# Merging two store transfers into one, a sixth load buffer, and a new fixed order of every engine, in a fused retention and gated feed-forward kernel

## The chip, the cores and the metric

The kernel runs on one core of a Trainium2 chip. The metric is device time in microseconds (us), the median of several executions. The profile is one execution taken by the hardware profiler; its span is about 1 to 2 us shorter than the time of the same run.

Engines are called PE (TensorE matmul), PEld (its weight loads), DVE (VectorE), ACT (ScalarE), POOL (GpSimd) and SP (the queue that issues transfers). An "h_ps" group is the first feed-forward matmul of one tile of 128 tokens, an "o_ps" group the second; there are 36 tiles. An eviction copies a matmul's result into a buffer (o_sb is that of the output). A store or load lands when its completion is reported. The chain is the work that ended last, followed back step by step to what released it. The granted clock is the share of its full clock that PE was allowed.

## The reference

```python
# retention: B=8, H=8, S=576, D=64
scores = (1/8) * q @ k^T
ret    = scores * Dmat           # causal, gamma_h ** (i - j)
x      = (ret @ v), heads side by side        # 4608 tokens x 512
# feed-forward
h    = x @ w_in                                # 512 -> 1024
solu = h * softmax(h)
ln   = (solu - mean) / sqrt(var + 1e-6) * g_ln
out  = ln @ w_out                              # 1024 -> 512, fp32
```

Inputs and the output are fp32: 32.7 MB are read and 9.4 MB written.

## The kernel before

Every instruction is an "op" with an engine, a duration, its dependencies and the buffers that it takes. For each engine a list (`FIRST`) fixes the order of the first 80 to 130 ops; the rest follow a periodic key. A small list scheduler turns this into one program order. So each engine works through a fixed order, and an engine that stands at one op stands with all that follow.

A load takes two neighbouring rows into one partition, so a tile's 128 tokens come out with the parity `j` slow and the pair index `q` fast: row `64*j + q` of the output tile belongs at row `2*q + j` in memory. The store undoes that, by two transfers per full tile, one for each parity:

```python
CAP = dict(raw=5, ..., xT=5, h=1, e=2, oc=2, solu=3, ..., o=1, osb=3)   # buffers
...
def x_ev(i):                                   # xT: the transposed tokens that h_ps reads
    nc.scalar.copy(out=d["xT"].rearrange("p c h q -> p c (h q)"), in_=d["av"][:, :, 0:256])

def o_ev(t):                                   # evicts o_ps into osb, the buffer of the store
    nc.scalar.activation(out=d["osb"], in_=..., func=ACT.Copy, scale=...)

def store(t):
    for j in range(2):
        q_dma = nc.scalar if t == NT - 1 and j else nc.sync
        if wi < 2:                             # a full tile: 32 of the 36
            r0 = b * S + 256 * wi + P * c
            q_dma.dma_start(
                out=out[r0 : r0 + P, :].rearrange("(q j) m -> j q m", j=2)[j],
                in_=tk[t]["osb"][64 * j : 64 * j + 64],
            )
        else: ...                              # cut: the 4 tail tiles, four pieces each
```

The softmax here doesn't subtract the row's maximum and nothing guards it: scores larger than these inputs give would overflow.

## Time and profile before

| | before |
|---|---|
| time, median | 225.9 us |
| span of the profile | 224.9 us |
| PE busy, share of the span | 207.0 us, 92% |
| a half-tile store, issue to landing | 2.4 us |
| ACT waiting with an o_sb eviction for a store | not among its waits |

Page of the kernel before: span and busy times, the rows of 40 slices for PE, the granted clock and DMA, the packet counts, the main DMA queue, the chain, and the stores' line of the DMA issues (KB each, us to landing).

```profile
span 224.9 us, 7378 instructions
PE 207.0 (92%) x2985; PEld 121.8 (54%) x2985; DVE 181.5 (81%) x320; ACT 163.2 (73%) x238; POOL 151.8 (67%) x231
...
PE   7776989899699999699999999999999999999991
...
PEclk9999999999999999999999999999999999999998
DMA  6999999995576610799988776777763552222324
...
DMA packets 65635, 42.64 MB, mean 190 GB/s; under 512 B 4024, under 2 KB 59456, under 8 KB 65600
...
q1 hardware_dynamic: 65200, 41.96, 66.9%
...
PE 63%; DVE 17%; DMA 9%; POOL 4%; issue 2%; SPq 2%; ACT 1%; DVEq 0%; POOLq 0%; ACTq 0%
...
out_dram<-o_sb SPq DMA_DIRECT2D x64, 128.0 KB, 2.4
```

PE is busy for 90% or more of each of the last 28 slices but two: the second half is at PE's limit. The chain that ended last is mostly PE's. Gaps are in the first half. The table of windows says so with numbers; the columns are the stretch, its length, busy time (instructions) of each engine, granted clock, DMA share and GB/s:

```profile
43.90:111.40 67.50, 63.32 (x973) 38.41 (x971) 63.96 (x104) 52.74 (x77) 57.16 (x81) 1.00 0.68 187
111.40:201.00 89.60, 89.60 (x1379) 55.12 (x1377) 75.67 (x136) 69.64 (x102) 64.55 (x103) 1.00 0.62 168
```

### The profile page before, as it was taken

What the parts mean: (1) busy time and instruction counts of PE and PEld (TensorE: products, weight loads), DVE (VectorE), ACT (ScalarE), POOL (GpSimd) and SP (SyncE); (2) the same over time, 40 slices, a digit from 0 to 9 for tenths busy, and PEclk for the clock granted to TensorE, in tenths of its full rate; (3) what the DMA queues carried; (4) which work ended last, traced back from release to release, by engine and by line L of the source; (5) the groups of instructions that cost most, each with busy time, mean ns of one, the idle gap of its engine ahead of it and who ended that gap; (6) DMA issues with size and microseconds to landing.
All of it is one profiled execution on the core that took longest, in us unless ns stands there. A gap on an engine that the chain in (4) does not pass through costs nothing.

```text
span 224.9 us, 7378 instructions
## 1 busy us (share of the span) xinstructions
PE 207.0 (92%) x2985; PEld 121.8 (54%) x2985; DVE 181.5 (81%) x320; ACT 163.2 (73%) x238; POOL 151.8 (67%) x231
## 2 busy tenths in 40 slices
PE   7776989899699999699999999999999999999991
PEld 2433445556455556465666666665666666555440
DVE  6654788999999998999999888888887888876540
ACT  3555889776869988578787777777777777776751
POOL 3429599899989989829578869695968677311010
PEclk9999999999999999999999999999999999999998
DMA  6999999995576610799988776777763552222324
GB/s 176 360 344 348 320 262 287 286 279 157 128 224 173 195 24 13 188 305 293 267 235 247 215 195 192 214 191 191 218 184 109 153 131 52 50 47 60 84 69 119
DMA packets 65635, 42.64 MB, mean 190 GB/s; under 512 B 4024, under 2 KB 59456, under 8 KB 65600
## 3 DMA queue, kind: packets, MB, share of 16 engines
q1 hardware_dynamic: 65200, 41.96, 66.9%
q8 instruction: 23, 0.38, 0.8%
q10 hardware_dynamic: 400, 0.21, 0.5%
q14 instruction: 12, 0.10, 0.2%
HBM read 32.71 MB, written 9.44 MB: 187 GB/s over the span
## 4 chain that ended last, share of the span: by engine, by line
PE 63%; DVE 17%; DMA 9%; POOL 4%; issue 2%; SPq 2%; ACT 1%; DVEq 0%; POOLq 0%; ACTq 0%
PE h_ps L431 21%; PE o_ps L501 21%; PE xy L311 6%; PE tln L480 5%; PE tqk L291 4%; DMA qr<-in_q_dram 4%; DVE solu L451 4%; PE s_ps L346 4%; DVE bs L457 3%; DVE ret L379 3%; DMA vr<-in_v_dram 3%; DMA kr<-in_k_dram 2%; DVE oc L509 2%; SPq L259 2%; DVE w L465 1%
## 5 line engine op out<-in xcount | busy, mean ns | idle before, releaser
L431 PE MATMUL h_ps<-w_in_122,xT 128*128 128x512 f16 x288 | 68.0, 379 | 2.0 <-DVE solu L451 1.9
L451 DVE TENSOR_TENSOR solu<-h_ps,e_sb 128x1024 f16<-128x1024 f32 x36 | 43.9, 1219 | 13.4 <-ACT e_sb L444 13.2
L444 ACT ACTIVATE e_sb<-h_ps 128x1024 f32<-128x1024 f32 x36 | 36.8, 1022 | 18.2 <-PE h_ps L431 17.9
L457 DVE BATCH_NORM_STATS2 bs<-solu 128x6 f32<-128x512 f16 x72 | 46.0, 680 | 0.1
L379 DVE TENSOR_TENSOR ret<-s_ps,masks 128x1024 f16<-128x1024 f32 x36 | 43.7, 1215 | 0.6 <-PE s_ps L346 0.4
L299 ACT COPY qkT<-tqk 128x1024 f16<-128x1024 f16 x36 | 36.3, 1008 | 9.3 <-PE tqk L291 9.1
L431 PEld LDWEIGHTS <-xT 128*128 128x128 f16 x288 | 27.0, 98 | 29.1 <-issue 2.8
L501 PEld LDWEIGHTS <-lnT 128*128 128x128 f16 x288 | 25.9, 98 | 27.2
L488 ACT COPY lnT<-tln 128x1024 f16<-128x1024 f16 x36 | 36.2, 1005 | 3.5 <-PE tln L480 3.5
L501 PE MATMUL o_ps<-w2c_124,lnT 128*128 128x512 f16 x160 | 38.0, 380 | 0.0
L501 PE MATMUL o_ps<-w2g_123,lnT 128*128 128x512 f16 x112 | 26.5, 380 | 0.0
L419 ACT CAST xT<-xy 128x512 f16<-128x512 f32 x36 | 21.4, 594 | 6.6 <-PE xy L311 6.2
L404 POOL TENSOR_TENSOR g<-tt,small 128x128 f32<-128x128 f32 x32 | 13.4, 418 | 15.3 <-DVE tt L400 15.3
L480 PEld LDWEIGHTS <-solu 128*128 128x128 f16 x288 | 18.5, 98 | 8.7 <-DVE solu L451 1.7
L517 ACT ACTIVATE o_sb<-o_ps,rs 128x512 f32<-128x512 f32 x20 | 13.7, 687 | 12.7 <-PE o_ps L501 6.9
L480 PE MATMUL tln<-ident,solu 128*128 128x128 f16 x288 | 22.0, 219 | 0.9 <-DVE solu L451 0.9
L346 PE MATMUL s_ps<-qkT 64*64 64x128 f16 x576 | 14.9, 220 | 0.8 <-ACT qkT L299 0.7
L346 PEld LDWEIGHTS <-qkT 64*64 64x64 f16 x576 | 9.5, 107 | 4.6 <-ACT qkT L299 1.8
L395 DVE TENSOR_TENSOR g<-xy,g 128x128 f32<-128x128 f32 x16 | 4.6, 289 | 8.7 <-PE xy L311 5.2
L400 DVE TENSOR_TENSOR tt<-xy,g 128x128 f32<-128x128 f32 x32 | 9.3, 292 | 2.7 <-ACT xT L419 0.7
L509 DVE SCALAR_TENSOR_TENSOR oc<-nws,mv,o_ps 128x512 f32<-128x512 f32 x14 | 10.3, 738 | 0.2 <-PE o_ps L501 0.2
L517 ACT ACTIVATE o_sb<-oc,rs 128x512 f32<-128x512 f32 x14 | 10.2, 728 | 0.3 <-DMA qr<-in_q_dram 0.3
(507 smaller groups left out, 336.9 us busy)
## 6 DMA issues: line engine op xcount, KB each, us to landing
kr<-in_k_dram SPq DMA_DIRECT2D x32, 256.0 KB, 4.6
vr<-in_v_dram SPq DMA_DIRECT2D x32, 256.0 KB, 4.8
qr<-in_q_dram SPq DMA_DIRECT2D x32, 256.0 KB, 4.8
out_dram<-o_sb SPq DMA_DIRECT2D x64, 128.0 KB, 2.4
w_in_f<-in_moe_w_in_dram SPq DMA_DIRECT2D x4, 512.0 KB, 5.9
w_f<-in_moe_w_out_dram SPq DMA_DIRECT2D x4, 512.0 KB, 8.0
qr<-in_q_dram SPq DMA_DIRECT2D x16, 64.0 KB, 2.3
kr<-in_k_dram SPq DMA_DIRECT2D x16, 64.0 KB, 2.0
```

Of the source, the lines that this page charges most:

```text
L299: nc.scalar.copy(out=d["qkT"], in_=d["tp"])
L346: nc.tensor.matmul(out=sv[ee[c], e, hp, j], lhsT=qkT[ee[e], 1, hp, j, ee[c]], rhs=qkT[ee[e], 0, hp, :, ee[c]], start=True, stop=True,)
L379: nc.vector.tensor_tensor(out=d["ret"].rearrange("p e h j q -> p (e h) (j q)"), in0=d["s"].rearrange("p e h j q -> p (e h) (j q)"), in1=ma ...
L419: nc.scalar.copy(out=d["xT"].rearrange("p c h q -> p c (h q)"), in_=d["av"][:, :, 0:256])
L431: nc.tensor.matmul(out=h_ps[:, hh], lhsT=st[2 * w + dc // 2]["xT"][:, c, dc % 2], rhs=w_in16[:, dc, hh], start=(dc == 0), stop=(dc == 3),)
L444: nc.scalar.activation(out=d["e"], in_=d["h"], func=ACT.Exp, accum_out=ws[w]["se"][:, c : c + 1])
L451: nc.vector.tensor_tensor(out=d["solu"], in0=d["h"], in1=d["e"], op=ALU.mult)
L457: nc.vector.bn_stats(out=bs[:, half], in_=tk[t]["solu"][:, half * 512 : half * 512 + 512])
L480: nc.tensor.transpose(out=tp[:, c], in_=d["solu"][:, c * P : (c + 1) * P], identity=ident)
L488: nc.scalar.copy(out=d["lnT"], in_=d["tp"])
L501: nc.tensor.matmul(out=d["o"], lhsT=d["lnT"][:, c], rhs=(w2g16 if t < NE else w2c16)[:, c], start=(c == 0), stop=(c == 7))
L517: nc.scalar.activation(out=d["osb"], in_=d["oc"] if t < NE else d["o"], func=ACT.Copy, scale=ws[t // 2]["rs"][:, t % 2 : t % 2 + 1],)
```

## The change

Its intent: save the second issue of each full tile's store; let loads run further ahead (`raw` from 5 to 6); and replace the order by a new one, listed over the whole run instead of about the first half of each engine's ops. A transposing load of k is also in the code, but its threshold (`ND = 99`) leaves it unused.

```diff
-    CAP = dict(raw=5, qk16=3, v16=4, tp=1, qkT=3, s=1, ...
+    CAP = dict(raw=6, qk16=3, v16=4, tp=1, qkT=3, kT=3, s=1, ...
 FIRST = dict(
     PE=(
-        "G K0 T0 S0 T1 I0 V0 K1 S1 I1 V1 M1_0 T2 K2 S2 L0 I2 V2 K3 T3 M1_1 S3 WM ..."
+        "G T0 K0 S0 T1 I0 V0 K1 S1 I1 V1 M1_0 T2 K2 S2 T3 M1_1 I2 V2 K3 S3 L0 ..."
         ... (cut: all five engines, to the last op of the run)
     def store(t):
-        for j in range(2):
-            q_dma = nc.scalar if t == NT - 1 and j else nc.sync
-            if wi < 2:
-                r0 = b * S + 256 * wi + P * c
-                q_dma.dma_start(
-                    out=out[r0 : r0 + P, :].rearrange("(q j) m -> j q m", j=2)[j],
-                    in_=tk[t]["osb"][64 * j : 64 * j + 64],
-                )
+        if wi < 2:
+            r0 = b * S + 256 * wi + P * c
+            nc.sync.dma_start(
+                out=out[r0 : r0 + P, :].rearrange("(q j) m -> j q m", j=2), in_=tk[t]["osb"]
+            )
         ... (cut: the 4 tail tiles, four pieces each as before)
```

## The prediction

> **What bounds the kernel now.** TensorE. The page gives PE 207.0 of 224.9 us (92%) at full granted clock. In the table of windows PE is busy 89.6 of 89.6 us between 111.4 and 201 us; successive h_ps groups (one per 128-token tile, 36 in all) start 5.26 to 5.37 us apart there. No order of the same instructions shortens that stretch. PE idle, plus warm-up matmuls of zeros counted as busy:
>
> - 15.6 to 24.2 us (first to second h_ps): 2.5 + 1.2
> - 24.2 to 31.1: 1.0 + 0.6
> - 31.1 to 43.9: 0.9
> - 43.9 to 111.4: 4.2
> - 201 to the end: 5.4, of which 4.6 is the last eviction and store.
>
> About 11 us could go at best, none of it in the second half.
>
> **Why those gaps exist.** From 44 to 111 us VectorE is busy 64.0 of 67.5 us: it is the limit there, because the first 14 tiles need an extra pass (oc, 0.74 us). Part of that is blocking: the 2-column adds of line 468 take 0.16 us in the second half but 0.97 to 1.20 us at 47, 58, 92 and 104 us, when GpSimd is mostly busy. The Trainium skill (SBUF — State Buffer, "Who interferes with whom") says a VectorE instruction with two SBUF inputs contends with a GpSimd one reading SBUF; these durations agree. The largest PE wait (1.7 us at 92 us) follows such a pair (0.82 + 1.19 us), placed ahead of the mask that PE needed.
> Before 44 us loading sets the pace: DMA share is about 1.0, and GpSimd waits 2.6 us (at 14 to 17) and 1.5 us (at 26 to 28) for data.
>
> **What the change does.** Transfers: a full tile's two stores (1.11 us of issue together) become one. SP matters only where its in-order queue stands at stores: from 74 to 91 us it issues eight stores while DMA falls to 0.03 share; GpSimd later waits 4.0 us for a q load. The new order spreads stores among loads; the sixth buffer lets loads run further ahead. Neither is worth more than about 0.5 us directly. The DMA transpose code is dead (its threshold is 99). No work is removed, apart from about three warm-up matmuls.
>
> Order: the second h_ps now comes before the attention of tiles 2 and 3, so it should start near 22 us instead of 24.2, the third near 28 to 29 instead of 31.2. But one q load goes ahead of k4's, one more w_out transfer ahead of v3's, and between 31 and 44 us GpSimd has 11.7 of 12.8 us of work and ScalarE 10.9, so most of the lead is paid back: about 1 us (0 to 2.5) remains at the fifth h_ps. From 44 to 111 us better interleaving can win at most VectorE's idle and blocking: I take 2.3 us (0.5 to 3.5). Steady part: 0 to -0.3. End: within 0.5. Sum: about 3.7 us.
>
> **Predicted:** 222.3 us, 219.3 to 225.0 eight times in ten. Faster by over 2% (under 221.5): 0.37; within 2%: 0.61; slower: 0.02.
>
> **What would show it.** Second h_ps at 21.5 to 23 us; fifth within 41.5 to 44; fifth to seventeenth h_ps 64 to 66 us (67.45 now); the remaining nineteen intervals unchanged at 98.7 us ±0.7; no long SP stand at stores between 70 and 95 us.
>
> **What would make it wrong.** Faster: the early lead is kept because loads arrive sooner than GpSimd needs them, or VectorE's blocking vanishes. Slower: the order does not know the blocking by GpSimd or DMA queueing, and one engine standing at a late operand stops the others; or stalls appear in the now-fixed second half.

## The result, and the profile after

The changed kernel takes 282.8 us (median of 4 runs, 282.4 to 283.4) against 225.9 us. The ratio is 1.252, with a 95% interval of 1.248 to 1.256. Ratios here are the mean time of one kernel's runs over that of the other's of the same rounds, so not quite the ratio of the medians quoted.

Page of the changed kernel, the same lines as above:

```profile
span 281.6 us, 7301 instructions
PE 220.5 (78%) x2982; PEld 126.2 (45%) x2982; DVE 178.2 (63%) x320; ACT 163.5 (58%) x238; POOL 151.7 (54%) x231
...
PE   8588999929999665994269879899496899999600
...
PEclk9999999977999997999859997999779999999985
DMA  8999996585443453648424345664331111111122
...
DMA packets 64674, 42.63 MB, mean 151 GB/s; under 512 B 3064, under 2 KB 58496, under 8 KB 64640
...
q1 hardware_dynamic: 64240, 41.95, 49.2%
...
DMA 50%; PE 21%; SPq 10%; ACT 10%; issue 3%; POOL 2%; DVE 0%; ACTq 0%; POOLq 0%
DMA out_dram<-o_sb 38%; SPq L293 7%; PE o_ps L545 7%; PE h_ps L475 6%; DMA kr<-in_k_dram 5%; DMA w_f<-in_moe_w_out_dram 3%; DMA qr<-in_q_dram 3%; PE tqk L333 3%; ACT e_sb L488 2%; ACT lnT L532 2%; ACT qkT L342 2%; PE tln L524 2%; PE xy L354 2%; ACT o_sb L561 2%; DMA masks<-masks 2%
...
out_dram<-o_sb SPq DMA_DIRECT2D x32, 256.0 KB
```

The compute work is the same (ACT 163.5 us against 163.2; PE is busy for 13.5 us more, at a mean granted clock of 0.93), but half of the chain is now DMA, and stores are 38% of the chain. PE has holes until about the 225th us and at the end, and its granted clock dips around many of them. Yet the DMA row is emptier than before. The stores' line gives no time to landing here; landings below are those of the chain. The waits of ACT name the place (us in total, times, longest):

```profile
ACT o_sb L561 <- DMA out_dram<-o_sb: 55.1, 17, 8.6
```

One such hole, in the chain in order of time (start, length):

```profile
78.75 7.86 DMA qr<-in_q_dram
...
86.70 7.86 DMA out_dram<-o_sb
...
94.66 0.04 ACT o_sb L561
...
95.29 1.10 ACT e_sb L488 x2
96.39 0.41 ACT lnT L532
96.80 8.68 DMA out_dram<-o_sb
```

A store is issued at 86.70 us and lands at 94.56. Only then does ACT get an `osb` buffer (there are three), evict o_sb, and go on in its fixed order to the exponential and to lnT, for which PE waits. In this view the store takes 7.9 us, three times as long as each half before, for twice the bytes. The q load ahead of it in the chain takes 7.86 us too, against a median of 4.8 us before.

The chain does not say why it is slow. The packet line does. "Under 512 B" counts, beside small data, the 4-byte packets that report a transfer's completion. They fall by 4024 - 3064 = 960. With 16 of them for each of the 64 half stores of before and 2 for each of the 32 single stores of now, the fall is 64 × 16 - 32 × 2 = 960. So each single store ran on 2 DMA engines. The Trainium skill (DMA: Bandwidth & Descriptors, "Why a DMA increments its semaphore by 16 and not by 1") states the rule: such a transfer uses the largest number of engines, at most 16, that divides the slowest dimension of size above 1 on both sides, and each engine used posts one completion. The new store's output pattern is `j q m`, with j = 2 outermost. The old halves had q = 64 there.

The packet records say it a second way. I took every 2 KB packet from the first store's to the last one's (the w_out loads, whose packets have that size too, are over by then) and counted how many are in flight at once, as shares of that time:

```
in flight               0      1      2      3     4 to 13   14 to 17
before                65.3%   4.0%   1.5%   1.1%    14%        14%
changed kernel        23.0%   5.9%  62.3%   6.3%    1.7%       0.7%
```

The 2.4% with four or more come almost wholly from the tail tiles, whose pieces are cut as before. In the last stretch of the changed kernel, where nothing but stores flows, two or three are in flight nearly without a break. With packets of every kind counted (over 100 bytes, from the 30th us to the end), fewer than two are in flight for 1.3% of the time in the changed kernel and for 23.9% before: as it should be if two engines hardly ever rest. The records do not name the engine, so this is not a count per engine. It also fits the length of the run. The main queue takes 49.2% of 16 × 281.6 us, so 2217 engine-us. The full tiles' stores are 32 × 128 packets of 84 ns median, 344 engine-us, half on each of the two engines: 172 us. The rest, spread over 16, is about 117 us for each engine. An estimate from these: 172 + 117 = 289 us of work for each of those two engines, in a span of 281.6 us (a little too much; three store packets at once on two engines mean that the records of neighbouring packets overlap). By this estimate they are full, while the other 14 are busy for 117 us. It takes the loads to fill them: from 225 to 257 us, with the loads over, PE is busy 31.8 of 32 us in the changed kernel, so in that stretch stores alone on two engines keep up with PE.

### The profile page after: what moved, and what is told of

The parts are those of the page before. It is cut to its first block, busy times and chain, and to the rows that moved or that the text cites. A ratio compares the mean times of both kernels' runs of the same rounds, so it can differ in the third digit from the quotient of the medians.

```text
span 281.6 us, 7301 instructions
## 1 busy us (share of the span) xinstructions
PE 220.5 (78%) x2982; PEld 126.2 (45%) x2982; DVE 178.2 (63%) x320; ACT 163.5 (58%) x238; POOL 151.7 (54%) x231
## 2 busy tenths in 40 slices
DMA packets 64674, 42.63 MB, mean 151 GB/s; under 512 B 3064, under 2 KB 58496, under 8 KB 64640
## 3 DMA queue, kind: packets, MB, share of 16 engines
q1 hardware_dynamic: 64240, 41.95, 49.2%
## 4 chain that ended last, share of the span: by engine, by line
DMA 50%; PE 21%; SPq 10%; ACT 10%; issue 3%; POOL 2%; DVE 0%; ACTq 0%; POOLq 0%
DMA out_dram<-o_sb 38%; SPq L293 7%; PE o_ps L545 7%; PE h_ps L475 6%; DMA kr<-in_k_dram 5%; DMA w_f<-in_moe_w_out_dram 3%; DMA qr<-in_q_dram 3%; PE tqk L333 3%; ACT e_sb L488 2%; ACT lnT L532 2%; ACT qkT L342 2%; PE tln L524 2%; PE xy L354 2%; ACT o_sb L561 2%; DMA masks<-masks 2%
## 5 line engine op out<-in xcount | busy, mean ns | idle before, releaser
L475 PE MATMUL h_ps<-w_in_125,xT 128*128 128x512 f16 x288 | 70.7, 390 | 0.4 <-DVE solu L495 0.3
L545 PE MATMUL o_ps<-w2c_127,lnT 128*128 128x512 f16 x160 | 40.8, 401 | 1.7 <-ACT o_sb L561 0.9
L545 PEld LDWEIGHTS <-lnT 128*128 128x128 f16 x288 | 27.5, 102 | 30.9 <-issue 5.4
L475 PEld LDWEIGHTS <-xT 128*128 128x128 f16 x288 | 27.8, 100 | 29.3 <-issue 3.7
L545 PE MATMUL o_ps<-w2g_126,lnT 128*128 128x512 f16 x112 | 28.1, 397 | 0.0
L463 ACT CAST xT<-xy 128x512 f16<-128x512 f32 x36 | 21.2, 588 | 11.4 <-DVE tt L444 6.4
L524 PE MATMUL tln<-ident,solu 128*128 128x128 f16 x288 | 23.5, 227 | 4.7 <-ACT lnT L532 4.1
L437 DVE COPY g<-xy 128x128 f32<-128x128 f32 x16 | 4.6, 290 | 13.5 <-PE xy L354 13.3
```

The source lines that it names most:

```text
L475: nc.tensor.matmul(out=h_ps[:, hh], lhsT=st[2 * w + dc // 2]["xT"][:, c, dc % 2], rhs=w_in16[:, dc, hh], start=(dc == 0), stop=(dc == 3),)
L524: nc.tensor.transpose(out=tp[:, c], in_=d["solu"][:, c * P : (c + 1) * P], identity=ident)
L545: nc.tensor.matmul(out=d["o"], lhsT=d["lnT"][:, c], rhs=(w2g16 if t < NE else w2c16)[:, c], start=(c == 0), stop=(c == 7))
```

## The experiments

Theory T1: the single store runs on 2 engines because of its outermost size, and these two cannot carry the stores and their share of the loads. Rivals: T2, the new order itself makes engines stand; T3, one transfer per tile is slow because it is one (a larger piece that frees its buffer later). All runs of one batch share a chip. The kernel before took a median of 226.1 us beside the first four, 225.8 us beside the others.

### 1. Only the stores undone (a_two_stores)

```diff
 # changed kernel, store(): the two half-tile transfers of the kernel before
# (cut: the tail tiles' four pieces go back to their old order too)
-        nc.sync.dma_start(out=... "(q j) m -> j q m" ..., in_=tk[t]["osb"])
+        for j in range(2):
+            q_dma.dma_start(out=... "(q j) m -> j q m" ...[j], in_=tk[t]["osb"][64*j : 64*j+64])
```

> The changed kernel with only the stores put back to two transfers per full tile (one for even, one for odd output rows). Theory T1 (the single store names the row parity, of size 2, as its slowest dimension and so runs on 2 of the 16 DMA engines): 219 to 225 us, o_sb no longer waits for store DMA (55 us in the changed kernel, under 3 us here), TensorE clock back above 0.98. T2 (the new order itself makes engines stand): 270 us or more. T3 (one transfer per tile is slow because it is one, whatever its shape): 219 to 225 us.

Measured: 226.1 us, ratio to before 0.999 (0.995 to 1.003). The small packets are those of the kernel before again, 4024, and the o_sb wait for stores falls from 55.1 to 0.8 us (second line):

```profile
DMA packets 65634, 42.63 MB, mean 190 GB/s; under 512 B 4024, under 2 KB 59456, under 8 KB 65600
...
  DMA out_dram<-o_sb: 0.8, 2
```

So all of the 56.7 us between 282.8 and 226.1 us come from the store. T2 falls. My own number for the new order (219 to 225 us) fails too; section 6 takes that up.

### 2. Only the single store, on the kernel before (b_one_store)

```diff
 # kernel before, store(): the single transfer of the changed kernel
-        for j in range(2): ... two half-tile transfers
+        nc.sync.dma_start(out=... "(q j) m -> j q m" ..., in_=tk[t]["osb"])
```

> The kernel before with only the single store per full tile. T1 and T3: 260 us or more, with o_sb waiting for store DMA some 40 us or more and only about 0.13 DMA share while nothing but stores flows. T2: 225 to 227 us.

Measured: 290.6 us, ratio 1.284 (1.278 to 1.290); o_sb waits 55.2 us for stores. The small packets are as few as in the changed kernel, 3064:

```profile
DMA packets 64674, 42.63 MB, mean 148 GB/s; under 512 B 3064, under 2 KB 58496, under 8 KB 64640
```

The single store alone makes the loss, in either order. The DMA share that I named as a sign was a bad one. While only stores flow it is 0.14 on two engines (changed kernel, first line) and 0.14 on 16 (the changed kernel with a_natural's stores of section 3, second line):

```profile
225.00:257.00 32.00, 31.77 (x390) 17.99 (x387) 24.73 (x42) 23.99 (x35) 8.91 (x17) 1.00 0.14 54
...
190.00:210.00 20.00, 20.00 (x266) 11.59 (x265) 15.11 (x28) 14.85 (x21) 2.56 (x5) 1.00 0.14 50
```

The packets in flight are the sign.

### 3. One store per tile on 16 engines (a_natural, b_natural, a_outer16)

If tokens are put into natural order earlier, when xT is written, the output tile is one contiguous block and its single store has 128 rows outermost. The result is correct.

```diff
 def x_ev(i):
     nc.scalar.copy(
-        out=d["xT"].rearrange("p c h q -> p c (h q)"), in_=d["av"][:, :, 0:256]
+        out=d["xT"].rearrange("p c h (q j) -> p c h j q", j=2),
+        in_=d["av"][:, :, 0:256].rearrange("p c (h j q) -> p c h j q", h=2, j=2),
 def store(t):       # full tiles (cut: the tail tiles, two pieces each in place of four)
+        nc.sync.dma_start(out=out[r0 : r0 + P, :], in_=tk[t]["osb"])
```

> The changed kernel with the tokens put into natural order when xT is evicted (a permuted write on ScalarE), so that the output tile is one contiguous block and its single store has 128 rows as its slowest dimension. Same result. T1: 218 to 225 us, each store landing in 2 to 4 us, xT copy not over 0.65 us. T3: 265 us or more. T2: 270 us or more.

> The kernel before with natural token order (permuted xT copy) and so one 16-engine store per full tile. The issue of stores is not on the chain: 225.5 to 227.5 us; the xT copy at 0.74 us instead of 0.59 us, as in the same edit of the changed kernel. A gain of 1% or more would show that store issue mattered in the kernel before.

Measured: 227.7 us on the changed kernel (ratio 1.004, 0.999 to 1.009) and 227.4 us on the kernel before (1.004, 0.998 to 1.010). Stores of 256 KB land in 2.2 us. T3 falls: one transfer per tile is as good as two when it has 16 engines. It is not better. The chain of the kernel before has no store's issue in it; the dearer copy below could hide a small gain, but a_outer16 (section 5), which has one store per tile without that copy, takes 226.5 us and is no faster either. The permuted copy takes 0.74 us instead of 0.59, which I had expected to be free in the first of the two runs and had not priced.

The DMA issues' line for stores in the changed kernel with natural order:

```profile
out_dram<-o_sb SPq DMA_DIRECT2D x32, 256.0 KB, 2.2
```

### 4. Two transfers, cut the other way (a_col_halves)

```diff
 # changed kernel, full tiles: two transfers of 256 columns, each still "j q m"
+        for m in (slice(0, 256), slice(256, 512)):
+            nc.sync.dma_start(out=out[r0 : r0 + P, m].rearrange("(q j) m -> j q m", j=2),
+                              in_=tk[t]["osb"][:, m])
```

> The changed kernel with two transfers per full tile, cut by columns (256 each), each still naming the row parity first. T1: as slow as the changed kernel or slower, 278 us or more (same two engines, pieces of 1 KB instead of 2 KB). T3: 219 to 230 us, as with the two transfers of before. T2: about 282 us.

Measured: 292.1 us, ratio 1.290. Two transfers again, with the size 2 outermost, and as slow. What the two halves of before had was not their number but their outermost dimension.

### 5. The number of engines as a dose (a_outer4, a_outer8, a_outer16) and the number of buffers (a_osb12, a_outer4_osb12)

The row order is made wrong, so these three give a wrong result; the bytes, the 2 KB pieces and all else are those of the changed kernel. Only the outermost size differs.

```diff
-    out=out[r0 : r0 + P, :].rearrange("(q j) m -> j q m", j=2), in_=tk[t]["osb"]
+    out=out[r0 : r0 + P, :].rearrange("(q a) m -> a q m", a=4), in_=tk[t]["osb"]   # or 8, 16
```

> The changed kernel, still one 256 KB store per full tile and the same 2 KB pieces, but with 4 as the slowest dimension of its output pattern (output row 4q+a instead of 2q+j: the rows of a tile land in the wrong order on purpose, so the result is wrong). T1 as a matter of engine count: per engine about 117 us of other traffic plus half of the 2-engine store time of about 170 us, together near 203 us, under the span that TensorE needs: 226 to 234 us, hardly any o_sb wait for store DMA. If only 16 engines will do, or if the slowness is that of a single strided store: 265 us or more.

> One store per full tile with 8 as the slowest dimension (row order wrong on purpose). T1 by engine count: per engine about 117 us of other traffic plus 43 us of stores; between the 16-way form (226.5 us) and the 4-way form (242.4 us): 226 to 231 us.

> The same with 16 as the slowest dimension (row order wrong on purpose). T1: 225 to 227.5 us, like the changed kernel with two stores; store landing 2 to 3 us. If scattered rows in one transfer were the fault: 265 us or more.

| outermost size | time, us | ratio to before | packets under 512 B |
|---|---|---|---|
| 2 (the changed kernel) | 282.8 | 1.252 | 3064 |
| 4 | 242.4 | 1.069 | 3128 |
| 8 | 227.0 | 1.004 | 3256 |
| 16 | 226.5 | 1.000 | 3512 |

The small packets follow 3000 + 32 × size exactly, so the number of engines used is the outermost size, as the skill's page has it. Time falls with it. (One of the four runs with size 4 counts as slow; the fast ones take 241.2 to 242.9 us.) The scatter of the rows is not what costs: the median 2 KB packet of a store takes 84 ns with each of the four sizes. Eight are enough here; four are not, against my estimate of 226 to 234 us. The packet lines of the changed kernel with size 4 and with size 16:

```profile
DMA packets 64738, 42.63 MB, mean 177 GB/s; under 512 B 3128, under 2 KB 58560, under 8 KB 64704
```

```profile
DMA packets 65122, 42.63 MB, mean 189 GB/s; under 512 B 3512, under 2 KB 58944, under 8 KB 65088
```

More buffers tell lack of throughput from a wait that buffering could hide:

```diff
-               xT=5, h=1, e=2, oc=2, solu=3, sml=8, lnT=4, o=1, osb=3)
+               xT=5, h=1, e=2, oc=2, solu=3, sml=8, lnT=4, o=1, osb=12)
```

> The changed kernel with 12 instead of 3 buffers of o_sb. If two DMA engines lack throughput for stores plus their share of loads (about 117 + 172 us of work in a 282 us run): still 272 to 285 us, the waits moving from o_sb to load data and to the end. If it is only the latency of one store against three buffers: under 240 us.

> The 4-way store (242.4 us, above what I had expected) with 12 o_sb buffers. If four engines have throughput enough (about 203 us of work) and the loss was stores queued behind bursts of loads against three buffers: 225 to 231 us, no o_sb wait for store DMA. If four engines still lack throughput, in the loading half at least: 238 us or more, with waits for load data in place of the o_sb waits.

Measured with size 2: 282.9 us, as with three buffers. The waits of POOL for loads in that run (with three buffers they sum to 9.4 us for v, 7.3 for k and 8.4 for q):

```profile
POOL v L316 <- DMA vr<-in_v_dram: 31.2, 5, 15.2
...
POOL k L308 <- DMA kr<-in_k_dram: 16.9, 7, 4.9
POOL q L308 <- DMA qr<-in_q_dram: 9.4, 5, 5.4
```

ACT no longer waits for stores, and loads come late instead. By the rule cited above each load of 128 rows also has a sixteenth on each of the two full engines, and it has landed only when these have delivered; the records do not show this engine by engine. So the limit is the throughput of two engines, not the wait for a buffer.

Measured with size 4 and twelve buffers: 238.1 us against 242.4. So the buffers gave back 4 of the 16 us above the 16-engine form. The rest is again late loads (POOL waits 12.5 us for v). My estimate for four engines, 203 us of work in the run, is a mean over the run; that stretches of heavy loading exceed it fits the waits but was not measured per engine.

### 6. The new order and the sixth buffer (hyb_two, a_two_raw5)

With two stores the new order takes 226.1 us, no faster than before; I had predicted 222.3. Starts of the h_ps groups in the profiles divide the runs (us):

| | first h_ps | 1st to 5th | 5th to 17th | 17th to 36th | 36th to end | span |
|---|---|---|---|---|---|---|
| before | 15.63 | 28.30 | 67.45 | 98.67 | 14.85 | 224.9 |
| new order, two stores | 16.87 | 26.48 | 68.81 | 99.58 | 12.86 | 224.6 |
| new order in about its first half only | 15.85 | 27.64 | 67.65 | 98.67 | 14.89 | 224.7 |
| new order, two stores, five load buffers | 16.24 | 27.17 | 75.58 | 106.87 | 12.84 | 238.7 |

The last row's profile is of a slow run (240.7 us), and no profile of a fast one is kept.

In the new order PE has done one more o_ps group by the 17th h_ps (14 against 13), and so has one fewer to do after the 36th; a group is 1.73 us. Taking that out, the middle stretch gains 67.45 - (68.81 - 1.73) = 0.37 us and the end 14.85 - 12.86 - 1.73 = 0.26 us. The steady stretch loses 0.91 us. (The first h_ps is late in the second row because PE's clock was granted at half speed from 11 to 17 us in that execution; other runs of this order begin at 15.5 to 16.2 us.)

```diff
 # hyb_two: changed kernel with two stores; FIRST cut to the ops that the kernel before
 # also listed (94 of ACT's, 100 of DVE's, 129 of PE's, 102 of POOL's, 85 of SP's), in the new order
```

> The changed kernel with two stores per full tile and its new order kept only for those instructions whose order the kernel before fixed too; the rest by the periodic rule of before. If fixing the whole run costs what the profile shows (0.9 us more between the 17th and the 36th h_ps than before): that stretch back to 98.4 to 99.0 us and 225.0 to 225.9 us in all. If the two runs merely scatter: 99.3 to 99.9 us there and 226.0 to 226.4 us in all.

Measured: 226.6 us, ratio 1.002 (0.997 to 1.006). The steady stretch is back to 98.67 us, so its 0.9 us did belong to the new late order; but the end takes 14.89 us, and the total is the same. The expected 225.0 to 225.9 us fails, because I had not counted that the extra o_ps group goes back to the end.

Why the middle gave so little: the same stretch, 5th to 17th h_ps, in the kernel before, with the new order, and with the new order in about the first half only.

```profile
43.93:111.38 67.45, 63.27 (x971) 38.36 (x969) 63.91 (x104) 52.71 (x77) 57.12 (x81) 1.00 0.68 187
```

```profile
43.35:112.16 68.81, 65.73 (x981) 39.50 (x979) 62.35 (x106) 53.15 (x78) 61.83 (x89) 1.00 0.83 238
```

```profile
43.49:111.14 67.65, 63.62 (x971) 38.55 (x969) 60.62 (x105) 52.42 (x77) 57.48 (x83) 1.00 0.65 181
```

In the last of them DVE (third busy column) has 3.3 us less to do than before, since fewer of its small adds were blocked by POOL (3.7 us of blocking against 6.7 us, summed over the durations of the two small operations above their usual 0.11 and 0.16 us). The stretch is no shorter. So DVE's work is not shown to bound it, and this run speaks against it. PE leaves the least room: it is busy 63.3 of 67.45 us, so 4.2 us at best could go (that PE is the limit there was not tested by itself). Of these the new order removed 1.1 us of idle time, while its busy time, the extra group taken out, rose by 0.7 us.

The sixth buffer:

```diff
-    CAP = dict(raw=6, ...      # changed kernel with two stores
+    CAP = dict(raw=5, ...
```

> The changed kernel with two stores per full tile and five load buffers as before. If the sixth buffer contributes nothing: 226.0 to 226.8 us, as with six. If the new order leans on it: 228 us or more, with GpSimd waiting for loads.

Measured: 239.3 us (median of 4; two of these runs count as slow, being over 1.5% above the fastest; the fast ones are 236.1 and 238.9, ratio 1.049). So the new order leans on the sixth buffer. The waits of SP's queue, in the profile of a slow run, suggest the way it happens:

```profile
SPq L293 <- POOL k L308: 20.8, 9, 10.2
SPq L293 <- POOL q L308: 12.6, 7, 3.8
```

A load stands at the head of the in-order queue until POOL frees a buffer, and the stores behind it stand too; ACT then waits 11.4 us for stores. No profile of a fast run of this form is kept, so the way is not shown for those.

No version beat the kernel before: 226.1 us (new order, six buffers, two stores) is the nearest, and is the same within the interval.

## Why the prediction was wrong

- **The step that failed** is "Neither is worth more than about 0.5 us directly", said of the merged store and the sixth buffer. I costed the store by its issue time on SP (1.11 us for two) and did not ask whether its landing would change. The runs show 56.7 us for the store alone on the new order (282.8 to 226.1 us) and 64.5 us on the old one (226.1 to 290.6). The output pattern's outermost size went from 64 to 2, and with it the engines from 16 to 2. The diff shows this: the `[j]` behind the rearranged pattern is gone, so j has become a dimension, and the outermost one. The skill's page states the rule; I did not look it up because I read the edit as a saving of issue time.
- The list of what would make the prediction wrong named DMA queueing only for the order. It did not ask which resource the store runs on.
- The sixth buffer: also mis-sized. The new order without it takes 239.3 us against 226.1 us with it. What it is worth in the old order was not run.
- **The middle stretch**, "I take 2.3 us (0.5 to 3.5)", was worth 0.37 us at equal PE work. The step behind it, "it is the limit there", said of VectorE, failed: in hyb_two three microseconds less of its work shortened nothing. A share of 95% busy did not show it to be the limit. The skill's rule on blocking (SBUF — State Buffer, "Who interferes with whom") does fit the 0.16 and 0.97 to 1.20 us of the same add; but in hyb_two 3.0 us less of such blocking did not shorten the stretch.
- The early part held: second h_ps predicted at 21.5 to 23 us, measured 21.74; third at 28 to 29, measured 28.27; fifth within 41.5 to 44, measured 43.41 (in the changed kernel, before its first stores pile up). The last range is a weak test: the kernel before, with 43.93, lies in it too. The total of 222.3 us would have failed without the slow stores as well (226.1 us).
- "The remaining nineteen intervals unchanged at 98.7 us ±0.7" failed: 126.1 us in the changed kernel, 99.6 us with two stores.
- The dips of the granted clock (mean 0.928) come with the holes in PE's work and go with them (0.98 or more in a_two_stores). How much of the 56.7 us they add was not separated; PE's busy time rose by 13.5 us.

## What to carry to other kernels

When transfers are merged or a pattern is rearranged, look at the outermost dimension of both sides before counting transfers: it sets how many DMA engines run it. Stores on two engines can delay the loads as well: with twelve buffers the waits moved from stores to loads. A nearly empty DMA row can hide two full engines; the count of small completion packets, or of packets in flight, tells it. And an engine that is busy 95% of a stretch is not shown to be its limit until taking work from it shortens the stretch.

## What the Trainium skill lacked or had wrong

- DMA: Bandwidth & Descriptors, "Rules for kernel authors", says of two transfers to disjoint partition halves to use one 128-partition transfer. Followed as it was here, that cost 25%: 282.8 us against 226.1 us for the two halves. The row lacks the condition that the merged pattern must keep 16 engines (the condition stands in the row "Use all 16 engines" of the same table, and is right: outermost 2, 4, 8, 16 gave 64, 128, 256, 512 completion packets for 32 stores). Two halves against one 16-engine store made no difference in time: 226.1 against 226.5 us.
- The same page gives no measurement of what transfers on few engines do to the others beside them: with 12 store buffers the time stayed at 282.9 us, and POOL waited 31.2, 16.9 and 9.4 us for v, k and q loads, against 9.4, 7.3 and 8.4 us with three buffers.
- SBUF — State Buffer, "Door 1: The DMA port swizzle", says that partitions 0 to 63 reach half of the ports. The traces fit it but do not test it: the median 2 KB packet of a half-tile store took 145 ns in the kernel before (118 to 145 ns in the four runs with such stores), that of a full-tile store in natural order 84 to 86 ns. Full-tile stores with outermost size 16 have slow packets too (a quarter of them 153 ns or more), so the half tile is not the only cause.
- No page that I read gives the cost of a permuted fp16 write on ScalarE (SBUF — State Buffer has only a general note on 16-byte lines): the xT copy of 128x512 elements took 0.59 us in order and 0.74 us when neighbouring elements were written 4 bytes apart.
